# Folding a one-row matmul into a full table, and padding a one-column operand, in a Fourier mixing stage

## The chip, the cores and the metric

The kernel runs on one NeuronCore of a Trainium2 chip. The metric is the device time of one execution in microseconds, taken as the median of several executions. Before the change three executions took 833.44, 835.06 and 837.93 us, so the median is 835.06 us.

The engines are named as the profile names them: PE is TensorE's matmuls, PEld its weight loads, DVE is VectorE, ACT is ScalarE, POOL is GpSimd, and SP is the queue that issues the DMAs.

## The reference

The reference has two blocks. The first is attention for 4 batches, 8 heads, 768 tokens and head size 64; each token sees a window of nearby tokens and one summary per block of 32. Its output, brought to `(4, 768, 512)`, is `x` of the second block:

```
X = fft(fft(x, axis=1), axis=2);  u = x + real(X)
un = (u - mean(u)) / sqrt(var(u) + 1e-6)
out = u + relu(un @ w_ch1) @ w_ch2          # 512 -> 2048 -> 512
```

The change concerns `real(X)`. A Fourier transform over 768 tokens and then over 512 channels is done as two matrix products with tables of cosines and sines; only the real part is needed: cosine times cosine minus sine times sine.

## The kernel before, in words

**Order of the work.** Batch 0's attention comes first (`first_attention`). For every batch `b` follow the Fourier mix (`gen_fourier`), the first product with ReLU (`gen_hidden`) and the second (`gen_out`), each in two halves `c`. The two products use a Strassen form with seven block products (`product`, L1171 and L1235). The function `drive` (L1301) interleaves the issue of several generators: the Fourier mix of batch `b + 1`, at a raised priority of 600, is mixed with the last `gen_out` of batch `b`; the attention of the next batch is mixed with the hidden products. A scheduler then fixes the order on each engine from its own estimates, so that on PE, DVE and ACT the pieces of two generators alternate in a fixed order. [...]

**Fold before the token transform.** By symmetry the tokens are folded in two (`sd`, DVE, from `x`), and the channels in two (`zw`) and again in two in `fold_ends` (L859). For each parity `par` of the output frequency this gives four groups of 128 channels in `fg`: group 0 even cosine, group 1 even sine, groups 2 and 3 the odd ones. One channel, number Q = 128, has no partner. It is copied to a small tile of its own, `zq`, with one column for each of the three token tiles (L868). The copies of `fold_ends` are done by POOL in batch 0 and by ACT in the other batches; its sums by DVE. `fg` and `zw` lie in one large buffer, `fold`, under the tag "u", which has only one buffer: it is also the place of the normalised input `u` of the hidden products, so a fold can start when the batch before has read its last `u`.

**Token transform.** In `gen_fourier`, for each `par` and each group `g`, three matmuls (L1072) over the three token tiles form `y`, 128 channels by 193 frequencies. In group 1 three more matmuls, L1076, put the lone channel's cosine transform into row 0 of the same PSUM tile: their weights are `zq[:, par, s2:s2 + 1]`, one column. Row 0 of group 1 is free, because the sine at channel 0 is zero. ACT copies every `y` twice (L1078 forward, L1079 mirrored) into `big`.

**Channel transform.** For batches 1 to 3, `mix_halves` (L1020) takes each of six token tiles: four matmuls of all 128 rows (L1029) with tables `e0` (129 columns), `e1` (128), `o0` (127) and `o1` (128), and one matmul, L1031, whose contraction has one row: row 0 of group 1, the lone channel, with the 129-column table `row`. They write even and odd columns of one PSUM bank `mx`. Four DVE additions then add `mx` to `x` (L562, called from L1033 to L1036), ACT forms the mean and the square sum (L1112, L1114), DVE the norm (L1123 to L1132), ACT and DVE in turn the normalised `un` (L1144, L1147), and PE transposes it (L1151, `unt`). Batch 0 takes another way through the channel transform (L1100, L1102), without L1031.

A matmul of 32-bit floats is shown as two passes, each with a weight load of its own, so 18 matmuls of L1031 (six tiles, three batches) are 36 passes, and 24 matmuls of L1076 (three tiles, two parities, four batches) are 48.

**Other users of POOL.** POOL does little: the copies of batch 0's fold, and the sums of `v` over blocks for batch 3 (L565), the last of which (`vbs`) wait for matmuls of the attention.

Of the kernel before, what the change touches and what calls it, by code (L numbers as in the profile page):

```python
# [9 lines left out]
FP = mybir.dt.float32  # L10
# [6 lines left out]
P = 128  # L17
# [405 lines left out]
def _tables(S, DM):  # L423

    g = _general_consts(S, DM)
    nb = S // BLOCK


    r, i, c = np.arange(96)[:, None], np.arange(S // QB)[None, :], np.arange(QB)[None, :]
    wide = np.ones((P, QB), dtype=np.float32)  # L430
    wide[0:96] = (r > c) & (r < c + 2 * W)
    count = np.zeros((P, S // QB), dtype=np.float32)
    count[0:96] = (QB * i - W + r >= 0) & (QB * i - W + r < S)
    count[96:96 + nb] = BLOCK

    r, i, c = np.arange(64)[:, None, None], np.arange(nb)[None, :, None], np.arange(BLOCK)[None, None, :]
    tok = BLOCK * i - W + r
    near = (r > c) & (r < c + 2 * W) & (tok >= 0) & (tok < S)
    near = np.concatenate([near, near]).astype(np.float32)


    sel = np.zeros((4 * nb, 2, 2, 2, 32), dtype=np.float32)
    half = np.zeros((2, 2, 32, 2), dtype=np.float32)
    for h in range(2):
        half[:, h, :nb, h] = 1.0
        for e in range(2):
            for pair in range(2):
                for n in range(nb):
                    sel[(2 * pair + e) * nb + n, pair, e ^ h, h, n] = 1.0

    fs = np.ascontiguousarray(np.moveaxis(g["fs"], 2, 0))


    fd = g["fd"].reshape(P, 6, DM // 2)
    n = DM // 4
    odd = fd[:, 1, 1:n].copy()
    odd[0] = 0.0
    fm = np.concatenate([fd[:, 0, 0:n + 1], fd[:, 3, 0:n], odd, fd[:, 4, 0:n], fd[:, 1, 0:n + 1]], axis=1)
    fm = np.ascontiguousarray(fm)
    return dict(wide=wide, near=near, sel=sel.reshape(4 * nb, 2, P), half=half.reshape(P, 2), count=count, fs=fs,  # L460
                fd=g["fd"], fm=fm, ident=g["ident"])
# [26 lines left out]
def _main_program(ctx, tc, q, k, v, moe_w_ch1, moe_w_ch2, out):  # L488


    nc = tc.nc
    B, H, S, D = q.shape
    DM = H * D
# [10 lines left out]
    F2 = S // 4  # L504
    HT = NST // 2
    HD = DM // 2
# [12 lines left out]
    spool = ctx.enter_context(tc.tile_pool(name="small", bufs=4))  # L519
# [65 lines left out]
    def add_blocks(gg):  # L585
        raw, vb = to_add[gg]
        n = BLOCK * D // 2
        while n > D:
            tt(raw[:, 0:n], raw[:, 0:n], raw[:, n:2 * n], ADD)
            n //= 2  # L590
        tt(vb, raw[:, 0:D], raw[:, D:2 * D], ADD)
# [219 lines left out]
    def first_attention():  # L811

        x = x_of[0] = bpool.tile([P, NST, DM], FP, tag="x", bufs=2, name="x_0")
        fold = bpool.tile([P, 7, 2, S2], FP, tag="u", name="fold_0").rearrange("p a k n -> p (a k n)")
        wt["fold"] = fold[:, 0:3 * HT * DM].rearrange("p (i t d) -> p i t d", i=3, t=HT)
        p = {0: wide_scores(0, 0, lambda: add_blocks(0))}
        prepare(0, 1)
        sum_values(0, 0)
        load(0, 3)
        for g in range(NP - 1):  # L820
            p[g + 1] = wide_scores(0, g + 1, (lambda: add_blocks(1)) if g == 1 else None)
            wide_values(0, g, p[g], x)
            load_values(*following(0, g, 2))
            for par in range(2):
                fold_sequence(par, g)
            if g == 0:
                get_tables(0)
            if g < NP - 2:
                prepare(0, g + 2)
                sum_values(0, g + 1)  # L830
            if g == NP - 3:
                load_raw(1)
                load(1, 0)
                load_raw(2)
                sum_values(0, g + 2)
        fold_halves(0, 0)
        wide_values(0, NP - 1, p[NP - 1], x)
        for par in range(2):
            fold_sequence(par, NP - 1)
            if par:  # L840
                fold_halves(par, 0)
            fold_halves(par, 1)
            fold_ends(0, par, wt["fold"][:, par], wt["fold"][:, 2 - 2 * par])
# [12 lines left out]

    zqs = {}

    def fold_ends(b, par, zw, fg):  # L859

        Q = DM // 4
        if par == 0:
            zqs[b] = spool.tile([P, 2, HT], FP, tag="zq", bufs=2, name=f"zq_{b}")

        copy = nc.scalar.copy if b else nc.gpsimd.tensor_copy
        copy(out=fg[:, :, 0:DM:HD], in_=zw[:, :, 0:DM:HD])
        tt(fg[:, :, 1:Q], zw[:, :, 1:Q], zw[:, :, HD - 1:Q:-1], ADD)
        copy(out=zqs[b][:, par], in_=zw[:, :, Q])  # L868
        nc.vector.memset(fg[:, :, Q:Q + 1], 0.0)
        tt(fg[:, :, Q + 1:HD], zw[:, :, 1:Q], zw[:, :, HD - 1:Q:-1], SUB)  # L870
        copy(out=fg[:, :, DM - 1:DM], in_=zw[:, :, HD + Q:HD + Q + 1])
        tt(fg[:, :, HD + 1:HD + Q], zw[:, :, HD + 1:HD + Q], zw[:, :, DM - 1:HD + Q:-1], SUB)
        marks["fold", b] = nc.vector.tensor_tensor(out=fg[:, :, HD + Q:DM - 1], in0=zw[:, :, HD + 1:HD + Q],
                                                   in1=zw[:, :, DM - 1:HD + Q:-1], op=ADD).ins
# [20 lines left out]
    wt, issued = {}, set()  # L895
# [124 lines left out]
    def mix_halves(ps, y, fm, xt, half):  # L1020

        Q = DM // 4
        e0, e1, o0, o1, row = (fm[:, a:z] for a, z in ((0, Q + 1), (Q + 1, HD + 1), (HD + 1, HD + Q),
                                                      (HD + Q, DM), (DM, DM + Q + 1)))
        for out, g, table, last in ((ps[:, 0:HD + 1:2], 0, e0, False), (ps[:, 1:HD:2], 2, e1, True),
                                    (ps[:, HD + 2:DM:2], 1, o0, True), (ps[:, HD + 1:DM:2], 3, o1, True)):
            nc.tensor.matmul(out, y[:, g], table, start=True, stop=last, skip_group_check=True)  # L1029
            if not last:  # L1030
                nc.tensor.matmul(out, y[0:1, 1], row[0:1], start=False, stop=True, skip_group_check=True)  # L1031
        low, high = xt[:, 1:HD], xt[:, HD + 1:DM]
        tt(xt[:, 0:HD + 1], ps[:, 0:HD + 1], xt[:, 0:HD + 1], ADD)  # L1033
        tt(high, ps[:, HD - 1:0:-1], high, ADD)
        tt(low, low, ps[:, HD + 1:DM], SUB if half else ADD)
        tt(high, high, ps[:, DM - 1:HD:-1], ADD if half else SUB)  # L1036

    def gen_fourier(b):
        x = x_of[b]
        Q = DM // 4  # L1040
        fs, fd = tables[b] if b in tables else get_tables(b)
# [2 lines left out]
        bank = abank if b else dense_bank  # L1044
        if b:
            fold = bpool.tile([P, 7, 2, S2], FP, tag="u", name=f"fold_{b}").rearrange("p a k n -> p (a k n)")
            fold = fold[:, 0:3 * HT * DM].rearrange("p (i t d) -> p i t d", i=3, t=HT)
        else:
            fold = wt["fold"]
        fgs = [fold[:, 2 - 2 * par] for par in range(2)]  # L1050
        for par in range(2 if b else 0):
            sd, zw = fold[:, 0], fold[:, 1]
# [5 lines left out]
        zq = zqs[b]  # L1058
# [8 lines left out]
        for par in range(2):  # L1067
            for g in range(4):
                ps = bank([P, F2 + 2], f"y_{b}_{par}_{g}")
                y = ps[:, par:par + F2 + 1]  # L1070
                for st in range(HT):
                    nc.tensor.matmul(y, fgs[par][:, st, P * g:P * (g + 1)], fs[par][:, g % 2, st, :],  # L1072
                                     start=(st == 0), stop=(st == HT - 1))
                    if g == 1 and st == 0:
                        for s2 in range(HT):
                            nc.tensor.matmul(ps[0:1, par:par + F2 + 1], zq[:, par, s2:s2 + 1],  # L1076
                                             fs[par][:, 0, s2, :], start=False, stop=False, skip_group_check=True)
                nc.scalar.copy(out=ty[:, g, par:S2:2], in_=y[:, 0:F2])  # L1078
                nc.scalar.copy(out=tr[:, g, par:S2:2], in_=ps[:, F2:0:-1])  # L1079
                yield  # L1080
# [4 lines left out]
        for half in range(2):  # L1085
# [5 lines left out]
            for i in range(HT):  # L1091
                t = HT * half + i
# [3 lines left out]
                else:  # L1096

                    ps = bank([P, 2, HD], f"mx_{b}_{t}")
                    for par in range(2):
                        nc.tensor.matmul(ps[:, par, :], yt[:, half, 2 * par, cols], fd[:, 3 * par, :],  # L1100
                                         start=True, stop=False)
                        nc.tensor.matmul(ps[:, par, :], yt[:, half, 2 * par + 1, cols], fd[:, 3 * par + 1 + half, :],  # L1102
                                         start=False, stop=True)
# [14 lines left out]
            y, z = norm[:, 0], norm[:, 1]  # L1118
# [21 lines left out]
        for t in range(NST):  # L1140
            half, i = divmod(t, HT)
            y, shift = norms[half]
# [6 lines left out]
            ps = bank([P, 2, 2, P], f"unt_{b}_{t}")  # L1149
            for d in range(NDT):  # L1150
                nc.tensor.transpose(ps[:, d // 2, d % 2, :], un[:, t, P * d:P * (d + 1)], ident)  # L1151
            (nc.vector.tensor_copy if t % 2 else nc.scalar.copy)(
                out=u[:, half:half + 3:2, :, P * i:P * (i + 1)], in_=ps)
# [119 lines left out]
    ps = bank([P, 512], "warm")  # L1273
# [19 lines left out]
    for vw in vw_bufs:  # L1293
        nc.gpsimd.tensor_copy(out=vw[:, :, D].rearrange("p (e n) -> p e n", e=2),
                              in_=count[:, None, :].to_broadcast([P, 2, NQ]))
# [46 lines left out]
    for b in range(B):  # L1342
# [9 lines left out]
        last = gen_out(b, 1)  # L1352
# [4 lines left out]
        if b == B - 2:  # L1357
# [9 lines left out]
            ps = bank([1, 1], "flag_ps")  # L1367
# [42 lines left out]
```

## Time and profile before

| What | Value |
|---|---|
| Median of three executions | 835.06 us (833.44 to 837.93) |
| Profiled execution: span from first to last instruction | 833.5 us; the page has no other time for it |
| Mean granted TensorE clock | 0.992 |
| PE busy | 803.7 us, 96% |
| DVE, ACT, POOL busy | 487.5, 254.9, 16.1 us |
| L1072, wide matmuls of the token transform | x192 passes, 37.9 us busy |
| L1076, one-column matmuls | x48 passes, 10.4 us busy |
| L1029, wide matmuls of the channel transform | x144 passes, 27.0 us busy over three shapes |
| L1031, one-row matmuls | x36 passes, 7.9 us busy |

How to read it: matmuls overlap in the pipeline and their ends are modelled, so the busy time of a group is more than what it adds to the span. What a pass costs is read from the distance between the starts of consecutive passes in the timeline. The timeline merges consecutive instructions of one kind into one line: start, length from the first start to the last end, engine, line, operation, output and inputs, shape, and their number; a bracket shows idle time of the engine before them and what ended it. A shape such as "1*128" is the rows times the columns of the weights in the array.

### The profile page before, as it was taken

To read this page: it belongs to the slowest core of one execution; us is meant where nothing else is said; L and a number is where in the kernel's file an instruction comes from. 1 tells how busy PE (TensorE), PEld (TensorE's weight loads), DVE (VectorE), ACT (ScalarE), POOL (GpSimd) and SP (SyncE) were. 2 spreads that over 40 slices of the span, in tenths; PEclk is the share of its full clock that TensorE was granted. 3 is DMA by queue.
4 is the path that set the end of the run, shared out by engine and by line. 5 is a ranking of instruction groups with operands and counts; after the bars stand their busy time and mean duration, and the time that the engine had idled before them with its cause. 6 is when DMAs were issued, how large, how long until landed. Compare 5 with 4: busy or idle time off the path is not lost.

```text
span 833.5 us, 14698 instructions
## 1 busy us (share of the span) xinstructions
PE 803.7 (96%) x6074; PEld 577.3 (69%) x6074; DVE 487.5 (58%) x1117; ACT 254.9 (31%) x561; POOL 16.1 (2%) x27
## 2 busy tenths in 40 slices
PE   8978998999999999999999999999999999999997
PEld 5757655445578855886568875787667875786586
DVE  5778998977978553543376823542357833532351
ACT  3543756444635023203234213121323502101200
POOL 0010000000000200020000000000000000000000
PEclk9989999999999999999999999999999999999999
DMA  9997697978733277247443253423312235205001
GB/s 227 216 252 146 193 246 253 289 244 259 241 108 110 83 268 200 83 77 254 101 92 103 82 208 122 127 38 131 121 46 89 71 108 209 89 1 220 1 26 54
DMA packets 101612, 120.55 MB, mean 145 GB/s; under 512 B 50560, under 2 KB 83552, under 8 KB 101344
## 3 DMA queue, kind: packets, MB, share of 16 engines
q1 hardware_dynamic: 100848, 119.31, 48.6%
q8 instruction: 50, 0.82, 0.4%
q10 hardware_dynamic: 688, 0.20, 0.1%
q14 instruction: 26, 0.21, 0.1%
HBM read 96.96 MB, written 22.54 MB: 143 GB/s over the span
## 4 chain that ended last, share of the span: by engine, by line
PE 83%; DVE 10%; ACT 3%; issue 1%; DMA 1%; ACTq 0%; DVEq 0%
PE hx L1173 18%; PE ox L1237 17%; PE hz L1173 9%; PE oz L1237 8%; PE y L1072 4%; PE o L1214 4%; PE hy L1173 4%; PE oy L1237 4%; PE mx L1029 2%; PE sc L757 2%; DVE x L562 1%; PE unt L1151 1%; PE y L1076 1%; ACT qt L696 1%; PE av L790 1%
## 5 line engine op out<-in xcount | busy, mean ns | idle before, releaser
L1173 PE MATMUL hx<-u,w 128*128 128x384 f32 x512 | 186.2, 491 | 7.2 <-DVE h L562 3.3
L1173 PEld LDWEIGHTS hx<-u,w 128*128 128x128 f32 x512 | 94.5, 190 | 72.1 <-DVE h L562 7.0
L1173 PE MATMUL hz<-u,w 128*128 128x384 f32 x256 | 93.3, 487 | 0.0
L1237 PE MATMUL ox<-w,s 128*128 128x256 f32 x336 | 81.5, 381 | 0.3
L1237 PE MATMUL oz<-w,s 128*128 128x256 f32 x336 | 80.7, 379 | 0.0
L1237 PE MATMUL ox<-w,h 128*128 128x256 f32 x336 | 78.4, 381 | 0.4 <-DVE x L562 0.4
L1173 PEld LDWEIGHTS hz<-u,w 128*128 128x128 f32 x256 | 48.4, 190 | 34.3 <-ACT h L1190 1.1
L562 DVE TENSOR_TENSOR x<-ox,x 128x256 f32<-128x256 f32 x84 | 35.3, 421 | 62.1 <-PE ox L1237 62.0
L1237 PEld LDWEIGHTS ox<-w,h 128*128 128x128 f32 x336 | 63.2, 190 | 11.1 <-DVE x L562 1.5
L1237 PEld LDWEIGHTS oz<-w,s 128*128 128x128 f32 x336 | 63.5, 190 | 8.4
L1237 PEld LDWEIGHTS ox<-w,s 128*128 128x128 f32 x336 | 62.5, 190 | 9.2 <-DVE x L562 1.1
L562 DVE TENSOR_TENSOR h<-hx,h 128x384 f32<-128x384 f32 x32 | 17.7, 555 | 67.4 <-PE hx L1173 67.4
L1183 ACT COPY h<-hx 128x384 f32<-128x384 f32 x32 | 15.3, 477 | 127.3 <-PE hx L1173 115.6
L562 DVE TENSOR_TENSOR h<-hy,h 128x384 f32<-128x384 f32 x32 | 17.8, 556 | 60.6 <-PE hy L1173 57.4
L1173 PE MATMUL hy<-u,w 128*128 128x384 f32 x128 | 46.6, 487 | 0.0
L1214 PE MATMUL o<-w,h 128*128 128x512 f32 x96 | 42.6, 596 | 1.2 <-DVE w L562 1.2
L1237 PE MATMUL oy<-w,h 128*128 128x256 f32 x168 | 39.8, 379 | 0.0
L1199 ACT ACTIVATE h<-hx 128x384 f32<-128x384 f32 x32 | 15.7, 489 | 78.7 <-PE hx L1173 78.6
L1072 PE MATMUL y<-fs,fold 128*128 128x193 f32 x192 | 37.9, 344 | 0.1
L1072 PEld LDWEIGHTS y<-fs,fold 128*128 128x128 f32 x192 | 32.1, 195 | 6.3 <-issue 4.9
L1173 PEld LDWEIGHTS hy<-u,w 128*128 128x128 f32 x128 | 24.2, 190 | 17.1 <-DVE w L562 0.6
L1237 PEld LDWEIGHTS oy<-w,h 128*128 128x128 f32 x168 | 31.9, 190 | 4.3
(141 smaller groups left out, 1073.2 us busy)
## 6 DMA issues: line engine op xcount, KB each, us to landing
w<-dw SPq DMA_DIRECT2D x44, 896.0 KB, 5.1
words<-in_moe_w_ch_dram SPq DMA_DIRECT2D x32, 512.0 KB, 6.6
dw<-w SPq DMA_DIRECT2D x12, 896.0 KB, 6.8
vw<-in_v_dram SPq DMA_DIRECT2D x47, 192.0 KB, 5.2
kn<-in_k_dram SPq DMA_DIRECT2D x16, 384.0 KB, 4.5
qn<-in_q_dram SPq DMA_DIRECT2D x16, 384.0 KB, 5.1
out_dram<-x SPq DMA_DIRECT2D x24, 256.0 KB, 2.0
fs<-c_fs SPq DMA_DIRECT2D x8, 579.0 KB, 3.5
```

The lines of the kernel that those rows point to most:

```text
L562: nc.vector.tensor_tensor(out=out, in0=in0, in1=in1, op=op)
L696: nc.scalar.copy(out=dst[D * e:D * (e + 1), s:S:2], in_=ps[D * s:D * (s + 1)])
L757: nc.tensor.matmul(ps[h][r:r + 64, i, :], kt[rows, o:o + 64], qt[rows, o:o + BLOCK], start=True, stop=True)
L790: nc.tensor.matmul(av[r][32 * j:32 * (j + 1), t, :], p[rows, h, i - NB2 * h, :], vw[rows, i, :], start=(t == 0), stop=False, skip_group_ch ...
L1029: nc.tensor.matmul(out, y[:, g], table, start=True, stop=last, skip_group_check=True)
L1072: nc.tensor.matmul(y, fgs[par][:, st, P * g:P * (g + 1)], fs[par][:, g % 2, st, :], start=(st == 0), stop=(st == HT - 1))
L1076: nc.tensor.matmul(ps[0:1, par:par + F2 + 1], zq[:, par, s2:s2 + 1], fs[par][:, 0, s2, :], start=False, stop=False, skip_group_check=True)
L1173: nc.tensor.matmul(ps, w[:, a, kk, :], u[:, r, kk, :], start=start and kk == 0, stop=stop and kk == 1, skip_group_check=True)
L1183: nc.scalar.copy(out=c11, in_=X)
L1199: nc.scalar.activation(out=c21, in_=X, func=AF.Relu)
L1214: nc.tensor.matmul(ps, h[:, n, hf, P * t:P * (t + 1)], wt[2, b, j][:, 2 * hf:2 * hf + 2, :], start=(n, hf) == (0, 0), stop=(n, hf) == (NC ...
L1237: nc.tensor.matmul(ps, left[a][:, n, :], wt[2, b, j][:, r, :], start=start and n == 0, stop=stop and n == NC - 1, skip_group_check=True)
```

## The change

There are two edits, and a place for the data.

- The table `fm` is put together anew. The one-row table `row` becomes a block of 128 rows with zeros outside row 0, and stands beside the odd sines, so that the two form one table `eo` of 129 + 127 = 256 columns. Both multiply group 1. `mix_halves` then has four matmuls for each token tile in place of five: 129, 256, 128 and 128 columns. The sum of the columns stays 641, as does the size of `fm`. [...]
- `zq` gets 128 columns for each parity and token tile, with the lone channel in column 0 and zeros in the others. L1076 then has weights of 128 by 128 and writes the whole of `y`. The zeros are written once for each batch by a new POOL memset of 128 x 768 elements (`fold_ends`, for `par` 0), ahead of the copy into column 0. The place is the unused rest of the `fold` buffer (`split_fold`), in place of a small tile of its own.

In the built program, POOL has four more instructions, which are the memsets: batch 0's right after the copies of `count` at the start (L1294), batch 1's right after batch 0's fold, batch 2's between the last two sums of L565 and batch 3's after the last of them. On ACT the copy of L868 waits for the memset too, and on PE the first of the padded matmuls. The order on DVE, ACT and SP is as before, but for one copy of `unt_3` on DVE that moves behind two other DVE operations in two batches; on PE the transposes of `unt_3` and `unt_4` in these two batches alternate, and stand behind one more matmul of L1237.

```diff
@@ _tables
-    fm = np.concatenate([fd[:, 0, 0:n + 1], fd[:, 3, 0:n], odd, fd[:, 4, 0:n], fd[:, 1, 0:n + 1]], axis=1)
+    row = np.zeros((P, n + 1), dtype=np.float32)
+    row[0] = fd[0, 1, 0:n + 1]
+    fm = np.concatenate([fd[:, 0, 0:n + 1], row, odd, fd[:, 3, 0:n], fd[:, 4, 0:n]], axis=1)
@@ first_attention, and the same in gen_fourier for the other batches
-        wt["fold"] = fold[:, 0:3 * HT * DM].rearrange("p (i t d) -> p i t d", i=3, t=HT)
+        wt["fold"] = split_fold(0, fold)
@@ new
+    def split_fold(b, fold):
+
+        n = 3 * HT * DM
+        zqs[b] = fold[:, n:n + 2 * HT * P].rearrange("p (r t m) -> p r t m", r=2, t=HT)
+        return fold[:, 0:n].rearrange("p (i t d) -> p i t d", i=3, t=HT)
@@ fold_ends
         if par == 0:
-            zqs[b] = spool.tile([P, 2, HT], FP, tag="zq", bufs=2, name=f"zq_{b}")
+            nc.gpsimd.memset(zqs[b], 0.0)
...
-        copy(out=zqs[b][:, par], in_=zw[:, :, Q])
+        copy(out=zqs[b][:, par, :, 0], in_=zw[:, :, Q])
@@ mix_halves
-        e0, e1, o0, o1, row = (fm[:, a:z] for a, z in ((0, Q + 1), (Q + 1, HD + 1), (HD + 1, HD + Q),
-                                                      (HD + Q, DM), (DM, DM + Q + 1)))
-        for out, g, table, last in ((ps[:, 0:HD + 1:2], 0, e0, False), (ps[:, 1:HD:2], 2, e1, True),
-                                    (ps[:, HD + 2:DM:2], 1, o0, True), (ps[:, HD + 1:DM:2], 3, o1, True)):
-            nc.tensor.matmul(out, y[:, g], table, start=True, stop=last, skip_group_check=True)
-            if not last:
-                nc.tensor.matmul(out, y[0:1, 1], row[0:1], start=False, stop=True, skip_group_check=True)
+        e0, eo, e1, o1 = fm[:, 0:Q + 1], fm[:, Q + 1:3 * Q + 1], fm[:, 3 * Q + 1:4 * Q + 1], fm[:, 4 * Q + 1:5 * Q + 1]
+        nc.tensor.matmul(ps[:, 0:HD + 1:2], y[:, 0], e0, start=True, stop=False, skip_group_check=True)
+        for out, g, table in ((ps[:, 0:DM:2], 1, eo), (ps[:, 1:HD:2], 2, e1), (ps[:, HD + 1:DM:2], 3, o1)):
+            nc.tensor.matmul(out, y[:, g], table, start=False, stop=True, skip_group_check=True)
@@ gen_fourier
-                            nc.tensor.matmul(ps[0:1, par:par + F2 + 1], zq[:, par, s2:s2 + 1],
-                                             fs[par][:, 0, s2, :], start=False, stop=False, skip_group_check=True)
+                            nc.tensor.matmul(y, zq[:, par, s2], fs[par][:, 0, s2, :], start=False, stop=False, skip_group_check=True)
```

More of the change, by code (lines that the diff above doesn't have):

```diff
@@ L1046, in gen_fourier @@
             fold = bpool.tile([P, 7, 2, S2], FP, tag="u", name=f"fold_{b}").rearrange("p a k n -> p (a k n)")
-            fold = fold[:, 0:3 * HT * DM].rearrange("p (i t d) -> p i t d", i=3, t=HT)
+            fold = split_fold(b, fold)
         else:
```

## The prediction

> **What bounds the kernel now.** I read the page first: whether one engine is full, and which engine the chain that ended last runs on.
>
> ```profile
> span 833.5 us, 14698 instructions
> ...
> PE 803.7 (96%) x6074; PEld 577.3 (69%) x6074; DVE 487.5 (58%) x1117; ACT 254.9 (31%) x561; POOL 16.1 (2%) x27
> ...
> PE 83%; DVE 10%; ACT 3%; issue 1%; DMA 1%; ACTq 0%; DVEq 0%
> ```
>
> PE is full and carries 83% of the chain. The change works in the Fourier stages, so next I read the busy time of the stretches that hold them for batches 1, 2 and 3 (after the stretch: busy us of PE, PEld, DVE, ACT, POOL, then clock and DMA).
>
> ```profile
> 230.00:275.00 45.00, 44.81 (x247) 37.54 (x246) 36.69 (x97) 18.70 (x54) 0.00 (x0) 1.00 0.30 103
> ...
> 425.00:470.00 45.00, 44.49 (x344) 36.87 (x343) 36.13 (x99) 18.16 (x53) 0.32 (x1) 1.00 0.37 99
> ...
> 620.00:665.00 45.00, 44.87 (x346) 37.37 (x345) 37.01 (x102) 18.18 (x53) 0.00 (x0) 1.00 0.24 81
> ```
>
> PE idles less than 0.6 us in each 45: time taken off PE there comes off the span, unless another chain is just behind. Then the timeline of the weight loads in the channel transform of batch 1.
>
> ```profile
> 250.91 1.86 PEld L1029 LDWEIGHTS mx<-fm,big 128*128 128x128 f32 x16
> 252.90 0.29 PEld L1031 LDWEIGHTS mx<-fm,big 1*128 1x128 f32 x2
> 253.31 0.74 PEld L1029 LDWEIGHTS mx<-fm,big 128*128 128x128 f32 x6
> 254.18 0.29 PEld L1031 LDWEIGHTS mx<-fm,big 1*128 1x128 f32 x2
> 254.59 0.74 PEld L1029 LDWEIGHTS mx<-fm,big 128*128 128x128 f32 x6
> ```
>
> Sixteen wide loads start (1.86 - 0.19) / 15 = 0.111 us apart (0.19 is the last one's own length). From one one-row load to the next, 252.90 to 254.18, is 1.28 us for two one-row passes and six wide ones, where eight passes in steady flow would take 0.89. So each stay in the one-row shape costs 0.39 us beyond its passes, in the two switches. [...] The same for the one-column operand in the token transform:
>
> ```profile
> 243.08 0.52 PEld L1072 LDWEIGHTS y<-fs,fold 128*128 128x128 f32 x3
> 243.83 0.09 PEld L1076 LDWEIGHTS y<-fs,zq 128*1 128x1 f32 x2 [0.23 <-issue]
> 244.24 0.30 PEld L1072 LDWEIGHTS y<-fs,fold 128*128 128x128 f32 x2 [0.33 <-issue]
> 244.77 0.41 PEld L1076 LDWEIGHTS y<-fs,zq 128*1 128x1 f32 x4 [0.23 <-issue]
> ```
>
> Wide passes of 193 columns are (0.52 - 0.19) / 2 = 0.165 us apart. From 243.83 to 244.77 is 0.94 us for two one-column and two wide passes, 0.66 in steady flow: 0.28 us for each stay. The price of the wider table is read from a 256-column stream of the same stage:
>
> ```profile
> 258.38 1.70 PEld L1237 LDWEIGHTS oz<-w,s 128*128 128x128 f32 x8
> ```
>
> (1.70 - 0.19) / 7 = 0.216 us for a pass.
>
> [...] The trace has a six-element POOL copy, which reads, at 1.33 us beside fold sums on DVE (0.20 elsewhere), and a small memset beside DVE at 0.14.
>
> **The row (L1031).** Removed: 36 passes of 0.111 = 4.0 us, and their stays. The row passes of two tiles that are worked together stand next to each other, so a batch has five stays, not six: 15 x 0.39 = 5.85. Added: 36 passes of group 1 grow from 127 to 256 columns, 36 x (0.216 - 0.111) = 3.8. Net gain 6.05 us.
>
> **The column (L1076).** The 48 passes stay, with the same moving columns and 0.165 us each; [...]. The stays go: three in each of batches 1 to 3, four in batch 0 (one for parity 0, three for parity 1): 13 x 0.28 = 3.65 us. Gross gain of both 9.7 us.
>
> **The memset.** By the 640-element memset of the start (0.63 us) it takes 0.76 us. Batch 1's stands at the head of POOL's queue from 54 us on, and starts when the last hidden product has read `u`, about 230.9. ACT's copy L868, which now waits for it, ran at 234.63. So 3 us of DVE folding hide it; in batches 2 and 3 more, since the fold started 4 us after the last hidden product. If that cover is gone, L868 is late, behind it in ACT's queue the copies L866 and L871, and then PE's first `y` (236.18). If the memset instead blocked the DVE sum beside it, the fold would be late by up to 0.76 us, nearly all seen by PE, since `y` follows the fold without slack. I take 0; the bounds are 0 and 3 x 0.76 = 2.3 us. Batch 2's memset stands ahead of a `vbs` sum that ran at 426.34, when `u` was free already; its reader comes after 470. No DMA is moved, and the table keeps its size.
>
> **Where gain stays behind.** PE gains about 3 us by the end of a batch's channel transform; what feeds PE does not all move with it.
>
> ```profile
> 467.02 1.09 PE L1151 MATMUL unt<-ident,big 128*128 128x128 f32 x8 [0.38 <-ACT big L1144]
> ```
>
> The transposes already wait here for `un` in batch 2, and in 1 and 3 they come without slack. The chain from `mx` over DVE sums, ACT's two activations for each of six tiles and the norm moves up with PE where it waits for `mx` (DVE waited 1.54 us for the last tile, so there is room), but ACT's part, nearly unbroken from 254.8 to 262.6, moves up only by about 2.2 of 3 us. DVE is late after ACT by 0.5 to 0.9 us anyway, so most of that is covered, and one more matmul stands ahead of `unt_3` in two batches. I take 0.2 us for a batch (bounds 0 and 0.8): 0.6. The last group of the first tile waits for ACT's copy of the last `y`, 0.1 a batch: 0.3. In batch 1 the first pass of parity 1 follows its fold by a hair, so the 0.28 gained ahead of it is lost: 0.25 (bound 0.75, all batches). Batch 0's four stays, 1.1 us, are followed by a stretch in which DVE is busy 146 of 160 us; I count 60%, so 0.45 is lost (bounds 0 and 1.1). Sum 1.6 us.
>
> **Sum.** 9.7 - 1.6 = 8.1, taken as 8.0 us: 833.5 - 8.0 = 825.5 for the span of the profiled execution. The median of the runs shown is 1.5 us above that span, and I carry this over: 827.0 us. Bounds: with no losses 825.4; with all at their worst, 9.7 - 4.55 = 5.1, so 829.9; with the blocked fold too, 832.2. Three runs spread over 4.5 us, so a median may stray by 1.5. Half a per cent, 4.2 us, is about what this measurement can tell from no change.
>
> **Rivals.** First, the chain through ACT and DVE sets the pace: for it speaks the 0.38 us wait above, against it DVE's 1.54 us wait for `mx`. PE would then keep the token transform's gain and a third of the channel transform's, 2.5 + 2.0 = 4.5 us: 830.5. Second, the change doesn't do what it says: the stalls come from something else than the shape, say from adding into a PSUM range just written, and stay. Then what is left is 4.0 - 3.8 = 0.2 us: 834.9. Against it, the wide passes also add into the range just written, at 0.111 and 0.165 us. Third, on the slower side: the memset is starved, as POOL's six-element copy was, and gets no turn while DVE folds without a break. Place: ACT's queue at L868, then `y`. The cover ends at about 236 us in batch 1; every us later is a us of PE. It decides from 2.7 us a batch (8.0 / 3); if the memset waited until the fold's end near 240, PE would lose 4 us a batch, 12 in all: 839.1. Against it: it reads nothing, and in batches 2 and 3 it has 4 us more.
>
> **Chances.** My forecast 0.73, the first rival 0.16, the second 0.07, the third 0.04. Of the first rival a little over a third lies within half a per cent, the second wholly: faster 0.83, same 0.13, slower 0.04. The range, 823.5 to 832.5, holds the forecast, its bounds and the first rival.
>
> **What would show it.** Right: in the timeline, loads of `y` and `mx` with no idle time before the lone channel's passes, about 0.165 apart, and mean spacing in `mx` of 0.111 and, for the 256-column pass, 0.216; POOL memsets of 0.76 us that end before L868; PE with about 36 passes fewer; the stretches between the batches' first `mx` shorter by about 2.5 us each. Wrong: waits of PE for `fold` or `unt` that grow by more than 0.5 us a batch, a DVE fold sum beside the memset longer than 1.75 us, or a lower granted clock.

## The result, and the profile after

| | Kernel before | Changed kernel |
|---|---|---|
| Median of six executions each | 837.15 us (833.44 to 837.93) | 828.88 us (823.57 to 833.24) |
| Ratio | | 0.9907, 95% interval 0.9879 to 0.9936 |
| Profiled execution: its time, its span | span 833.5 us | 829.18 us, span 827.4 us |
| Mean granted TensorE clock | 0.992 | 0.987 |

The changed kernel is faster by 8.3 us, and the interval, applied to 837.15, allows 5.4 to 10.1 us. The profile page of the changed kernel, the same rows as were read before:

```profile
span 827.4 us, 14641 instructions
...
PE 798.8 (97%) x6038; PEld 583.6 (71%) x6038; DVE 486.9 (59%) x1117; ACT 254.6 (31%) x561; POOL 20.0 (2%) x31
...
PEclk9969999999999999999999999999999999999999
...
PE 81%; DVE 10%; ACT 5%; DMA 2%; issue 1%; POOL 0%; SPq 0%; DVEq 0%; ACTq 0%; POOLq 0%
```

PE has 36 passes fewer (6074 to 6038), POOL four instructions more, and PE is still the full engine, with 81% of the chain that ended last. In the third slice of the clock row the granted TensorE clock is 0.6 of full speed, where it was 0.8 before. This comes back below.

The weight loads of the channel transform of batch 1, changed kernel (start, length, engine, line, what, shape, number):

```profile
252.49 0.53 PEld L1034 LDWEIGHTS mx<-fm,big 128*128 128x128 f32 x4
252.94 1.84 PEld L1036 LDWEIGHTS mx<-fm,big 128*128 128x128 f32 x12
254.70 0.73 PEld L1241 LDWEIGHTS ox<-w,s 128*128 128x128 f32 x4
255.46 0.41 PEld L1034 LDWEIGHTS mx<-fm,big 128*128 128x128 f32 x2
255.78 0.96 PEld L1036 LDWEIGHTS mx<-fm,big 128*128 128x128 f32 x6
```

Every operand is 128*128 and no group starts late. The last six loads are two with 256 moving columns and four with 128. From 255.78 to the last of their starts is 0.96 - 0.19 = 0.77 us for five steps; two of 0.216 and three of 0.111 make 0.765. Nothing is left over for a stall. The same for the token transform:

```profile
244.28 0.95 PEld L1077 LDWEIGHTS y<-fs,fold 128*128 128x128 f32 x6 [0.30 <-issue]
245.21 0.35 PEld L1081 LDWEIGHTS y<-fs,fold 128*128 128x128 f32 x2
245.53 0.35 PEld L1077 LDWEIGHTS y<-fs,fold 128*128 128x128 f32 x2
245.86 0.68 PEld L1081 LDWEIGHTS y<-fs,fold 128*128 128x128 f32 x4
```

The lone channel's passes (L1081) now follow at 0.16 to 0.17 us each, without the gaps of 0.23 and 0.33 us that stood around them. The 0.30 us ahead of the first line is PE waiting for the fold of parity 1: the line says only "issue", but the first sum of that fold runs on DVE from 243.50 for 0.55 us, to 244.05.

The busy time in the stretches from the first token transform to the first hidden product, changed kernel, batches 1, 2 and 3 (columns as before: the stretch, its length, busy us of PE, PEld, DVE, ACT, POOL, then clock and DMA):

```profile
238.00:289.00 51.00, 50.94 (x277) 45.66 (x277) 38.65 (x101) 17.11 (x49) 6.15 (x5) 1.00 0.26 92
434.60:484.70 50.10, 50.10 (x274) 45.01 (x274) 35.42 (x97) 17.10 (x49) 0.00 (x0) 1.00 0.24 78
625.50:676.30 50.80, 50.37 (x275) 44.86 (x274) 35.97 (x99) 17.10 (x49) 0.00 (x0) 1.00 0.23 77
```

PE still idles less than 0.5 us in 50, so PE's saving was the span's saving in these stretches. To say where the time went, the timeline of PE was cut at marks that both kernels have: the first pass of `y` of each batch, and its first hidden product. In us:

| Stretch | Before | Changed | Changed, repeated | Before, repeated |
|---|---|---|---|---|
| start to first `y` of batch 1 | 236.2 | 237.8 | 235.3 | 234.6 |
| batch 1, `y` to hidden | 53.75 | 51.15 | 51.15 | 53.75 |
| to first `y` of batch 2 | 144.9 | 145.6 | 144.9 | 144.1 |
| batch 2, `y` to hidden | 53.63 | 50.05 | 50.05 | 53.64 |
| to first `y` of batch 3 | 140.92 | 140.88 | 140.87 | 140.92 |
| batch 3, `y` to hidden | 53.11 | 50.78 | 50.79 | 53.12 |
| sum of the three `y` to hidden | 160.49 | 151.98 | 151.99 | 160.51 |
| span | 833.5 | 827.4 | 824.1 | 831.2 |

The three mix stretches repeat within 0.02 us and give 8.51 us. The stretch up to batch 1 and the one after batch 1's mix differ by 0.7 to 2.5 us between two executions of one and the same kernel. So the difference of two spans, 6.1 us here, says less than the three stretches do.

### The profile page after: what moved, and what is told of

Same layout as the page of the kernel before. It is cut to its first block, busy times and chain, and to the rows that moved or that the text cites. A ratio compares the mean times of both kernels' runs of the same rounds, so it can differ in the third digit from the quotient of the medians.

```text
span 827.4 us, 14641 instructions
## 1 busy us (share of the span) xinstructions
PE 798.8 (97%) x6038; PEld 583.6 (71%) x6038; DVE 486.9 (59%) x1117; ACT 254.6 (31%) x561; POOL 20.0 (2%) x31
## 3 DMA queue, kind: packets, MB, share of 16 engines
q1 hardware_dynamic: 100848, 119.31, 49.2%
## 4 chain that ended last, share of the span: by engine, by line
PE 81%; DVE 10%; ACT 5%; DMA 2%; issue 1%; POOL 0%; SPq 0%; DVEq 0%; ACTq 0%; POOLq 0%
PE hx L1177 18%; PE ox L1241 16%; PE hz L1177 9%; PE oz L1241 8%; PE o L1218 4%; PE y L1077 4%; PE hy L1177 4%; PE oy L1241 4%; PE sc L759 2%; PE mx L1036 2%; DVE x L564 1%; DVE w L564 1%; ACT qt L698 1%; PE y L1081 1%; PE qk L696 1%
## 5 line engine op out<-in xcount | busy, mean ns | idle before, releaser
L1241 PE MATMUL ox<-w,s 128*128 128x256 f32 x336 | 81.2, 381 | 0.4 <-DVE x L564 0.3
L1241 PE MATMUL oz<-w,s 128*128 128x256 f32 x336 | 80.7, 379 | 0.0
L1241 PE MATMUL ox<-w,h 128*128 128x256 f32 x336 | 78.3, 381 | 0.3 <-DVE x L564 0.3
L1241 PEld LDWEIGHTS ox<-w,h 128*128 128x128 f32 x336 | 63.3, 190 | 10.9 <-DVE x L564 1.4
L1241 PEld LDWEIGHTS ox<-w,s 128*128 128x128 f32 x336 | 62.7, 190 | 9.3 <-DVE x L564 1.2
L1241 PEld LDWEIGHTS oz<-w,s 128*128 128x128 f32 x336 | 63.4, 190 | 8.2
L1241 PE MATMUL oy<-w,h 128*128 128x256 f32 x168 | 39.9, 379 | 0.0
L564 DVE TENSOR_TENSOR x<-oz,x 128x256 f32<-128x256 f32 x42 | 17.8, 423 | 29.5 <-PE oz L1241 29.5
L1241 PEld LDWEIGHTS oy<-w,h 128*128 128x128 f32 x168 | 32.0, 190 | 4.3
```

The source lines that it names most:

```text
L564: nc.vector.tensor_tensor(out=out, in0=in0, in1=in1, op=op)
L1241: nc.tensor.matmul(ps, left[a][:, n, :], wt[2, b, j][:, r, :], start=start and n == 0, stop=stop and n == NC - 1, skip_group_check=True)
```

## The experiments

**The row alone, and the column alone.** The first kernel is the one before with the new table and the new `mix_halves` only; the second is the changed kernel with the old ones put back.

```diff
@@ row alone: the kernel before, with
+    row = np.zeros((P, n + 1), dtype=np.float32)
+    row[0] = fd[0, 1, 0:n + 1]
+    fm = np.concatenate([fd[:, 0, 0:n + 1], row, odd, fd[:, 3, 0:n], fd[:, 4, 0:n]], axis=1)
...
+        nc.tensor.matmul(ps[:, 0:HD + 1:2], y[:, 0], e0, start=True, stop=False, skip_group_check=True)
+        for out, g, table in ((ps[:, 0:DM:2], 1, eo), (ps[:, 1:HD:2], 2, e1), (ps[:, HD + 1:DM:2], 3, o1)):
+            nc.tensor.matmul(out, y[:, g], table, start=False, stop=True, skip_group_check=True)
@@ column alone: the changed kernel, with
...
+            if not last:
+                nc.tensor.matmul(out, y[0:1, 1], row[0:1], start=False, stop=True, skip_group_check=True)
```

> Only the row is folded into the 256-column table; the lone channel keeps its one-column operand. Shape theory (each stay in the one-row shape costs 0.39 us, and the merge itself is even, 4.0 us removed against 3.8 added): about 5.5 us faster, ratio 0.9935; the time from the first to the last start on mx falls by 2.0 us in each of batches 1 to 3, the time from the first y to the first mx stays at 12.06, 11.80 and 11.79 us. Pace theory (ACT and DVE set the pace): mx is 2.0 us shorter, but the time from the last mx to the first unt grows by 1 us or more a batch, and the gain is 2 to 3 us. Adding theory (the stall comes from adding into a range just written): under 0.5 us.

> Only the lone channel's operand is padded to 128 columns; the row stays a matmul of one row. Shape theory: 13 stays of 0.28 us less what batch 0 and the fold keep, about 3 us faster, ratio 0.9965; the time from the first y to the first mx falls by 0.85 us in batches 2 and 3 and by 0.6 in batch 1, where a pass waits for the fold; mx unchanged at 9.38 us. Adding theory: no change, since the padded passes add into the range just written as before.

The marks of these runs, with those of the next experiment. The first three columns add up the stretches of batches 1 to 3.

| Kernel | `y` to `mx` | `mx`, first to last start | `y` to hidden | Gain | Median, ratio to before |
|---|---|---|---|---|---|
| before | 35.64 | 28.14 | 160.49 | | |
| row alone | 35.65 | 22.11 | 154.26 | 6.23 | 828.56, 0.9901 (0.9873 to 0.9930) |
| column alone | 33.36 | 28.14 | 158.21 | 2.28 | 833.65, 0.9964 (0.9947 to 0.9981) |
| both, as changed | 33.34 | 22.11 | 151.98 | 8.51 | 828.88, 0.9907 (0.9879 to 0.9936) |
| both, row a matmul of its own | 33.46 | 22.35 | 152.54 | 7.95 | 826.76, 0.9883 (0.9857 to 0.9910) |

The two parts act in two different stages, and their gains add up: 6.23 + 2.28 = 8.51. The medians rank the kernels less finely than the stretches do, as the wide intervals say: the row alone has about the same median as both.

**Padding without merging.** Is it the fold into one table that gains, or only that the operand has 128 rows? Here the zero-padded row is multiplied as a fifth matmul of its own, of full size.

```diff
-        for out, g, table in ((ps[:, 0:DM:2], 1, eo), (ps[:, 1:HD:2], 2, e1), (ps[:, HD + 1:DM:2], 3, o1)):
-            nc.tensor.matmul(out, y[:, g], table, start=False, stop=True, skip_group_check=True)
...
+            if not last:
+                nc.tensor.matmul(out, y[:, 1], row, start=False, stop=True, skip_group_check=True)
```

> As the changed kernel, but the row stays a matmul of its own, with its zero rows, 128 rows by 129 columns: five matmuls for a token tile, none merged. Shape theory: the stall is gone with the one-row shape, so mx takes 7.4 to 7.5 us a batch against 7.37 merged and 9.38 before, and the whole is within 0.5 us of the changed kernel, ratio 0.9905. Merge theory (the gain comes from having fewer matmuls and no second addition into e0's columns): the gain of the row is lost, mx near 9 us a batch, ratio near 0.9965.

The weight loads of the padded row (L1039) in batch 1:

```profile
250.33 0.30 PEld L1039 LDWEIGHTS mx<-fm,big 128*128 128x128 f32 x2
250.56 0.75 PEld L1037 LDWEIGHTS mx<-fm,big 128*128 128x128 f32 x6
251.22 0.30 PEld L1039 LDWEIGHTS mx<-fm,big 128*128 128x128 f32 x2
```

From one pair to the next is 0.89 us, where it was 1.28 with one row. The stage of `mx` takes 7.45 us a batch, against 7.37 with the merged table and 9.38 with the one-row operand. This kernel has as many passes, with as many columns, as the kernel before; only the weights grew from one row to 128, and 1.93 of the 2.01 us are gone. The merge itself is worth 0.08 us a batch, near the 4.0 - 3.8 = 0.2 us for three batches that the prediction's counts give. The fifth matmul also adds into the PSUM range that has just been written, so that was not the cause of the stall.

**Which shapes stall.** In one kernel (a single execution, 834.20 us), batch 1 uses 32 rows for the row operand and 32 columns for the column operand, batch 2 uses 64 and batch 3 uses 96. Otherwise it is the kernel with the fifth matmul.

```diff
-                nc.tensor.matmul(out, y[:, 1], row, start=False, stop=True, skip_group_check=True)
+                nc.tensor.matmul(out, y[0:rows, 1], row[0:rows], start=False, stop=True, skip_group_check=True)
...
-                            nc.tensor.matmul(y, zq[:, par, s2], fs[par][:, 0, s2, :], start=False, stop=False, skip_group_check=True)
+                            m = 32 * b or P
+                            nc.tensor.matmul(y[0:m], zq[:, par, s2, 0:m], fs[par][:, 0, s2, :], start=False, stop=False,
+                                             skip_group_check=True)
```

> The row as a matmul of its own with 32, 64 and 96 rows (zero rows added) in batches 1, 2 and 3, and the lone channel's operand with 32, 64 and 96 columns in the same batches; batch 0 has 128 columns. If any operand smaller than the array brings the stall: mx 9.4 us in all three batches, and y to mx 12.05, 11.80 and 11.79. If [...] more than half counts as full: 9.4 and 12.05, 11.80 in batches 1 and 2, but 7.45 and 10.95 in batch 3. If only the very small operands stall: 7.45 everywhere.

The `mx` stage took 9.38, 9.39 and 7.45 us, the stretch `y` to `mx` 12.13, 11.96 and 10.95 us. So 32 and 64 rows stall as fully as one row does, 32 and 64 columns a little more than one column, and 96 doesn't stall at all. The weight loads in this kernel, batch 1 with 32 rows, then batch 3 with 96:

```profile
254.08 0.29 PEld L1039 LDWEIGHTS mx<-fm,big 32*128 32x128 f32 x2
254.50 0.74 PEld L1037 LDWEIGHTS mx<-fm,big 128*128 128x128 f32 x6
255.36 0.29 PEld L1039 LDWEIGHTS mx<-fm,big 32*128 32x128 f32 x2
...
643.24 1.87 PEld L1037 LDWEIGHTS mx<-fm,big 128*128 128x128 f32 x16
645.03 0.30 PEld L1039 LDWEIGHTS mx<-fm,big 96*128 96x128 f32 x2
645.25 0.75 PEld L1037 LDWEIGHTS mx<-fm,big 128*128 128x128 f32 x6
645.92 0.19 PEld L1039 LDWEIGHTS mx<-fm,big 96*128 96x128 f32 x1
```

From one pair of 32-row loads to the next is 1.28 us, exactly as with one row; from one pair of 96-row loads to the next is 0.89 us, which is eight steady passes. So the shape decides in this kernel: 64 rows or columns stall, 96 don't. Why the line falls there, and what goes on in TensorE during a stall, the runs don't show. By rows a stay among full-size passes costs 1.28 - 0.89 = 0.39 us. By columns it is 0.28 us with one column, 0.31 with 32 and 0.34 with 64: from one pair of loads to the next the weight loads take 0.94, 0.97 and 1.00 us, where 0.66 is steady flow.

**The memset's cover, worked out to its end.** The prediction cost the memset at nothing, because DVE's folding hides about 3 us. It is repeated eight times, then sixteen times, in each batch. This adds the repeated memsets only, which write the same zeros. Each kernel ran once (832.31 and 830.09 us), so only the stretches are read, not the times.

```diff
-            nc.gpsimd.memset(zqs[b], 0.0)
+            for _ in range(8):
+                nc.gpsimd.memset(zqs[b], 0.0)
```

> The changed kernel with the POOL memset of each batch issued eight times, 5.9 us in place of 0.74. Cover theory: in batch 1 it ends near 238.6 us by the changed kernel's clock of events, so ACT's copy of the lone channel (236.33 there) and the first y (237.84) come about 1.6 us late and PE idles for it; in batches 2 and 3 the fold starts 4 us later after the memset, so nothing is late; DVE's fold sums beside it keep 1.75 and 0.95 us. Starving theory: a memset beside the fold takes well over 0.74 us, or the fold sums grow, and all three batches lose time.

> The changed kernel with the memset issued sixteen times, 11.8 us. The scheduler places the padded passes later in batch 1 (after some twenty passes of the other groups), as it did ACT's copy with eight. Cover theory: in batch 1 the memset ends near 244.5 us, ACT waits for it with the copies of y behind, and PE loses about 2 us against the changed kernel between the first y and the first mx (11.45 us there); in batches 2 and 3 it ends 0.7 us or so after the padded passes are due (10.95 there): up to 1 us each. Starving theory: more than 0.86 us a memset, DVE's fold sums longer than 1.76 us.

First the changed kernel with a single memset, POOL and then ACT in the timeline:

```profile
232.72 0.74 POOL L871 MEMSET fold<- 128x768 f32 x1 [177.78 <-PE hx L1177]
425.82 0.74 POOL L871 MEMSET fold<- 128x768 f32 x1 [53.39 <-issue]
426.52 0.60 POOL L567 TENSOR_TENSOR vbs<-vb 96x64 f32<-96x64 f32 x1
616.93 0.74 POOL L871 MEMSET fold<- 128x768 f32 x1 [189.81 <-PE vs L782]
```

```profile
236.33 0.20 ACT L876 COPY fold<-fold 128x3 f32<-128x3 f32 x1 [3.30 <-DVE fold L564]
```

Batch 1's memset ends at 233.46, and the copy L876 that needs it starts at 236.33 and had waited for DVE: 2.9 us of cover were unused. The DVE sums beside the memset took 1.75 us each, as without it.

Eight memsets take 6.31 us and end at 238.81. My expectation of a PE 1.6 us late in batch 1 was wrong: `y` to `mx` stayed at 11.46 us there. The scheduler had planned the longer memset and put the copy that waits for it (L877 in this kernel) behind the two that don't. The ACT timeline with eight memsets:

```profile
236.92 0.20 ACT L875 COPY fold<-fold 128x6 f32<-128x6 f32 x1 [4.11 <-DVE fold L564]
237.03 0.19 ACT L880 COPY fold<-fold 128x3 f32<-128x3 f32 x1
238.84 0.20 ACT L877 COPY fold<-fold 128x3 f32<-128x3 f32 x1 [1.62 <-POOL fold L872]
```

The copy did wait 1.62 us for POOL, but its readers on PE start at 240.29, so nobody was late. Sixteen memsets (12.67 us in batch 1) do reach PE, though the scheduler moved work again. PE's timeline there, at the padded passes of batches 1 and 2:

```profile
244.07 1.25 PE L1082 MATMUL y<-fs,fold 128*128 128x193 f32 x6 [0.57 <-ACT fold L877]
...
436.69 1.25 PE L1082 MATMUL y<-fs,fold 128*128 128x193 f32 x6 [1.54 <-ACT fold L877]
```

The three mix stretches lose 0.36, 2.30 and 1.06 us, 3.7 in all, for 11 us more of memset in each batch. In batch 1 other matmuls of the same stretch moved ahead of `mx` and filled most of the time: `y` to `mx` grew from 11.45 to 14.91 us, and from the last `mx` to the hidden product it shrank from 32.32 to 29.22. No memset, of the sixteen and of the eight, took more than 0.87 us, and the DVE sums stayed between 1.750 and 1.759 us. So neither engine starves the other.

**Other shape changes in the kernel.** If each change of shape costs so much, fewer changes elsewhere should gain too. In the attention of batches 1 to 3 the 64*64 and 64*32 operands of the scores come in two groups, with other work between; here they are joined.

```diff
             p, pm = scores(b, g)
-            yield
             sum_scores(b, g, pm)
+            yield
```

> The changed kernel with the scores against the block sums issued directly after the scores of the same heads in batches 1 to 3, so that PE goes from the 64 x 64 shape to the 64 x 32 one and then back, in place of two stays among wide matmuls. The same theory of shape changes, tried elsewhere: twelve times one change fewer, 0.2 to 0.3 us each, 2 to 3.5 us faster than the changed kernel, ratio to the kernel before near 0.987. If a change between two small shapes costs as much, or ACT's exponentials then come at a worse time: no gain, 0.990 or more.

This missed. The median is 828.64 us, ratio 0.9895 (0.9857 to 0.9933), which can't be told from the changed kernel's. Between batch 2's mix and batch 3's the stretch shrank from 140.88 to 140.32 us; batch 3's own went from 50.78 to 50.51, which the kernel with eight memsets shows too. Where batch 1's attention runs, the joined kernel seems to have lost. From batch 0's first hidden product to batch 1's first `y` four profiles without half clock there (the kernel before twice, the row alone, the column alone) take 145.5 us, and the changed kernel with one stretch of 3.4 us of half clock takes 147.1 and 147.2. The joined kernel has no half clock there and takes 147.15 all the same; at 91 us PE waits 1.01 us inside the score passes, which run on without a break in the changed kernel's first repeat. So the order seems to have cost about 1.6 us in one place and gained 0.6 in another; there is one profile of it. Two groups of small shapes side by side still differ in shape, and whether a change between two small shapes costs less than one to full size was not measured by itself.

**What stirs the stretch before batch 1.** The clock row showed a slice at 0.6. When the timeline is cut finely, the granted clock of each profile is either full or half (1.00 or 0.50), and the half-clock stretches, but for one at the very end, last 3.4 us or a multiple of it: in the kernel before from 49.2 to 56.0 and 83.3 to 86.7 us, in the changed one from 44.8 to 58.4, 82.3 to 85.7 and 130.1 to 133.5. Within a profile their starts are whole multiples of 3.41 us apart: 34.1 us before, 37.5 and 47.8 in the changed kernel. PE waits twice for data between 41 and 50 us. In the changed kernel (2.53 and 1.95 us) the half clock starts after the first of the two waits, in the kernel before (3.02 and 1.42 us) during the second. In the 3.41 us before the first half clock PE was busy for only 0.93 us in the changed kernel (41.36 to 44.77) and for 0.85 us in the kernel before (45.80 to 49.20). To see whether the half clock follows from these idle times, 16 passes that nobody reads, of 128 columns, are put into each of the two. Nothing else is added.

```diff
         fold_halves(0, 0)
+        keep_busy(0)
         wide_values(0, NP - 1, p[NP - 1], x)
+        keep_busy(1)
...
+    def keep_busy(n):
+        ps = bank([P, P], f"busy_{n}")
+        for _ in range(8):
+            nc.tensor.matmul(ps, ident, ident, start=True, stop=True)
```

> The changed kernel with eight matmuls of the identity, whose result nobody reads, ahead of and behind the last attention product of batch 0, where PE idles 2 to 3 us twice between 41 and 52 us. Clock theory (the spread of the runs comes from stretches of half clock that follow these idle times): less half clock before 66 us than the 13.7, 6.8 and 3.4 us of the profiles of the changed kernel, y to mx of batch 0 near 10 us, and 1 to 3 us faster than the changed kernel, ratio near 0.987. If the clock falls there for another reason: half clock as before, and up to 1 us slower, since the added work may come late.

> The kernel with the filled idle times of batch 0 once more, beside the changed kernel. If the fill is worth the 2 to 3 us that its first median lay below the changed kernel: about 826 us where the changed kernel has 828 to 829, with no half clock before 66 us. If that was chance: no difference, or half clock before 66 us in this profile.

First the changed kernel in its second repeat, which ran beside the second run of this kernel, and then the kernel with the idle times filled, in its first run; PE in the timeline:

```profile
44.40 2.40 PE L743 MATMUL av<-vw,p 128*64 128x65 f32 x48 [3.64 <-DVE fold L564]
48.81 1.51 PE L696 MATMUL qk<-ident,kn 128*128 128x128 f32 x6 [2.01 <-DVE wide L564]
```

```profile
42.85 1.75 PE L743 MATMUL av<-vw,p 128*64 128x65 f32 x48
44.52 2.05 PE L853 MATMUL busy<-ident 128*128 128x128 f32 x16
46.90 0.85 PE L696 MATMUL qk<-ident,kn 128*128 128x128 f32 x6 [0.33 <-DMA kn<-in_k_dram]
```

The same six transposes take 1.51 us in one and 0.85 in the other, and the 48 passes 2.40 and 1.75. In both profiles with the filled idle times there is no half clock before 66 us, where all twelve other profiles of this case have a stretch of it that starts between 43.3 and 49.9 us; and the first `y` of batch 1 starts at 233.9 and 232.1, against 237.8, 235.3 and 239.7 in three profiles of the changed kernel. The medians are 825.85 us (ratio 0.9865, 0.9827 to 0.9903) and 824.77 us (0.9850, 0.9812 to 0.9888). The changed kernel had 827.94 (0.9911, 0.9876 to 0.9946) in its first repeat, taken earlier, and 828.96 (0.9891, 0.9839 to 0.9943) beside the second run. This is the fastest version, by 2 to 4 us in its medians against the changed kernel; since the intervals overlap, that it is faster than the changed kernel is likely and not settled. That the half clock before 66 us follows from those idle times, however, is what these lines and the two profiles show.

**Repeats.** The changed kernel was repeated twice and the kernel before once, with no edit, to see what an execution alone can move.

> The changed kernel once more, with a second profile. Shape theory: ratio 0.990 within its interval, and the sum of what row_only and col_only gain. The first y of batch 1 stood at 237.84 us against 236.18 before, while the stages behind it were shorter: if that was a chance of the clock in this execution, it moves again by about a us or two; if the change costs it, it stays 1.7 us late.

> The changed kernel on the same chip as the next one. Shape theory: ratio 0.990, stages of batches 1 to 3 as in its other profiles (mx 7.37 us).

> The kernel before, with a second profile. Clock theory: the stages of batches 1 to 3 come out within 0.1 us of the first profile (y to mx 12.05, 11.80, 11.79; mx 9.38), and what differs is the start and batch 0, by 1 to 3 us, with a different amount of half clock there. Ratio within 0.5% of 1.

The kernel before, repeated, gives 836.68 us, ratio 0.9986 (0.9960 to 1.0012). The mix stretches of all repeats agree within 0.02 us with their first profiles, and what differs is the stretch before batch 1 (234.6 and 236.2 us before; 235.3, 237.8 and 239.7 changed) and the one after its mix (144.1 to 145.6). The first goes with the length of half clock before batch 1's `y`: 10.2 us in both profiles of before and in the first repeat of the changed kernel (236.2, 234.6 and 235.3 us), 20.5 and 23.9 us in the other two (237.8 and 239.7). It isn't the whole of it: the two profiles of the kernel before have the same half clock and are 1.7 us apart at batch 0's first `y` (52.12 and 50.40), where one waits 3.02 us for the DMA of `kn` and the other 2.15. What moves the stretch after batch 1's mix stays open.

## Why the prediction was right, point by point

**The time.** 827.0 us was predicted, 828.88 measured, within the range. The predicted gain, 8.0 us, meets 8.3 of the medians. That these agree to 0.3 us is in part luck, since the interval of the measurement reaches from 5.4 to 10.1. The working is better tested on the three mix stretches: there the prediction had the row's 6.05, nine of the thirteen column stays (2.5), and losses of 1.15 (all but batch 0's 0.45), which is 7.4 us; measured were 8.51. A small slip: its bound without losses, 825.4, should read 825.3 (833.5 - 9.7 + 1.5).

**The row, 6.05 us.** Right: 6.0 us in the `mx` stage (three times 2.01), and 6.23 to the first hidden product. The price of a stay, 0.39 us, and the count of five a batch fit the shape experiment, where 32 and 64 rows cost 1.93 us a batch more than 96. The 0.111 us between wide loads is the spacing of passes of 128 moving columns; a load's own record is longer. In the kernel before it is 0.183 us in the mean for one row of 128 columns, 0.191 for 128 rows, and 0.085 for one column: in these three shapes it goes with the columns and hardly with the rows, so the one-row operand saved at most 0.008 us in a load.

**The column, 13 x 0.28.** Right: 0.85 us a batch in batches 2 and 3, and 0.60 in batch 1, where PE waits 0.30 us for the fold. The prediction had named that wait and its price, 0.25 us. That a padded pass would still take 0.165 us with its wider load was the author's estimate: the load's record grew from 0.085 to 0.208 us in the mean (L1076 before, L1081 after), and the passes follow at 0.16 to 0.17 us all the same. In batch 0 the stretch from `y` to `mx` went from 12.92 to 11.80 us, where both profiles have the same length of half clock: 1.1 us, as four stays give.

**Batch 0's 60%.** Not settled. At batch 1's first `y` the repeat of the changed kernel, with as much half clock as both profiles of before, stands at 235.3 us, between their 234.6 and 236.2. Nothing of the 1.1 us can be seen there, and it can't be excluded either, since one kernel differs from itself by 1.6 us at this point. That count starts before anything was changed. From batch 0's own first `y` to batch 1's it is 184.06 and 184.25 us in the two profiles of before, and 183.76 in that repeat, with 7.3, 7.6 and 7.3 us of half clock between: 0.3 to 0.5 us kept of 1.1, where the prediction counted 0.65. With so few profiles this is a hint, no more.

**The memset at 0.** Right: 0.74 us each (0.76 was worked out from the smaller one), with 2.9 us of cover left over and DVE's sums unchanged at 1.75 us. The third rival is thereby refuted. What the prediction had wrong is its picture that the order would stay as it is under a longer memset: it had every us beyond the cover as a us of PE, but the eight memsets cost PE nothing in batch 1, because the scheduler moves the waiting copy back, and sixteen cost 3.7 us in three batches.

**Losses through ACT, DVE and the transposes, 0.6, and the wait for `y`'s copy, 0.3.** This is the term that was mis-sized: a loss of 0.9 us predicted, in sum none measured. The time from the last `mx` to the first `unt` is the same before and after, 9.61, 8.75 and 8.75 us, so the chain up to there moved up with PE. In batch 2 the 0.38 us wait of the transposes has gone. PE's timeline there, changed kernel:

```profile
463.86 1.14 PE L1155 MATMUL unt<-ident,big 128*128 128x128 f32 x8
464.83 0.60 PE L1241 MATMUL oz<-w,s 128*128 128x256 f32 x2
465.41 0.66 PE L1155 MATMUL unt<-ident,big 128*128 128x128 f32 x4
```

The eight transposes no longer end an idle time; the changed order has one more matmul of L1241 ahead of them, as the prediction said, and this was cover enough. In batch 3 it was not. From the last `mx` to the hidden product the three batches took 32.31, 32.45 and 31.93 us before, and 32.32, 31.74 and 32.47 after: batch 2 gained 0.7 us more than its stages, and batch 3 gave up 0.5. The weight loads there, changed kernel:

```profile
656.50 0.42 PEld L1155 LDWEIGHTS unt<-ident,big 128*128 128x128 f32 x4 [0.54 <-ACT big L1148]
662.63 0.95 PEld L1241 LDWEIGHTS ox<-w,h 128*128 128x128 f32 x5 [0.69 <-DVE x L564]
```

Before, the load ahead of the same `ox` waited 0.40 us for DVE, and those of the last four transposes waited for nothing. So the predicted kind of loss, a wait for ACT or DVE, did occur in one batch and was more than made good in another. The column alone shows the same shift (31.83 and 32.56 us in batches 2 and 3), the row alone doesn't (32.35 and 31.84); why is open. The first rival, which had the chain through ACT and DVE set the pace in every batch and gave 4.5 us, is refuted by the 8.51 us.

**The second rival.** Refuted by the fifth matmul of full size: it adds into a range just written, and doesn't stall (0.89 us from one pair of its loads to the next, eight steady passes).

**The bridge from a span to a median.** The prediction carried over 1.5 us from the three times shown. With three more executions the median of before rose from 835.06 to 837.15 us, so two of the three times had been on the low side. That the error of 1.9 us in the predicted time is of this kind is only argued: between the two kernels the gain came out 0.3 us from the forecast.

**A sign of being wrong.** The prediction had named a lower granted clock, and the first profile has one, 0.987 against 0.992. It was an execution's own: the first repeat of the changed kernel has 0.993.

## What to carry to other kernels

On a full PE, look for weights of few rows or columns that stand alone between full-size ones: in this kernel each such stay cost 0.28 to 0.39 us beyond its passes, and zeros up to 128 rows or columns removed it at no price on PE that could be seen, since the passes here are spaced by their moving columns (0.111 us at 128, 0.165 at 193, 0.216 at 256). Keep the padded matmul as it is if merging is awkward; the merge gave 0.08 us a batch of the 2.01. To judge a change of one per cent, cut the timeline at marks that both kernels have: stretches that repeat within 0.02 us tell more than medians that stray by several us.

## What the runs showed of the hardware that was not expected

- Weights of 64 rows stall exactly like those of 32 or of one, and 96 not at all (`mx` stage 9.39, 9.38, 9.38 and 7.45 us). Columns behave alike, with 0.28, 0.31 and 0.34 us a stay for one, 32 and 64, and no stall at 96. Padding to 96 would have been enough; nothing between 64 and 96 was measured.
- Two idle times of about 1.4 to 3.6 us on PE, in a kernel that keeps PE 96% busy, cost half-clock stretches of 3.4 to 13.7 us, of different length in each execution. They are one thing seen to differ between executions of one kernel, beside the waits for DMAs themselves, and 32 passes that nobody reads, about 4 us of PE, kept them away before 66 us.
- A memset on POOL beside DVE's sums takes 0.73 to 0.74 us, but for one of 32 and one of 64 at 0.86, and leaves the sums at 1.75 us.
